# Two early expert items instead of four, six wide ones instead of four, and the last routing steps in larger portions

## The chip, the cores and the metric

The kernel runs on one core of a Trainium2 chip. Its engines work side by side, each through its own queue of instructions in order: TensorE (PE in the profile; PEld is its loading of weights), VectorE (DVE), ScalarE (ACT), GpSimd (POOL) and SyncE (SP). They wait for each other by semaphores. Transfers between DRAM and the on-chip memory are issued by SP (all the plain ones) and by GpSimd (those that take their addresses from a list: indirect ones, which gather or scatter rows). The metric is the device time of one execution in microseconds (us).

## What is computed

Two blocks behind each other. The first is a recurrence over 768 steps for 4 batches and 8 heads of 48 features; the second sends each of the 3072 rows to its two best of 8 experts.

```python
f = 1.0 / (1.0 + np.exp(-f_logit))
for t in range(S):
    state = f[:, :, t, :, None] * state + np.einsum('bhd,bhe->bhde', k[:, :, t], v[:, :, t])
    y[:, :, t] = np.einsum('bhd,bhde->bhe', q[:, :, t], state)
...
noisy_logits = x @ w_gate + np.log1p(np.exp(x @ w_noise)) * noise     # x: y as (3072, 384)
top2 = ...                                                            # the two largest of 8, softmax over them
for e in range(E):
    h = np.maximum(x[mask] @ w1[e], 0.0)                              # 384 -> 1024
    out[mask] += top2_w[mask, k, None] * (h @ w2[e])                  # 1024 -> 384
```

All of it is float32.

## The kernel before

**Attention.** The 768 steps are cut into 6 chunks of 128 (NCH), for 4 batches, so 24 blocks (NS). A loop runs over i from -3 to 25, and in each turn over seven stages that belong to different blocks (forget, scaled, scores, summed, output, decays, features). Each stage of each block is a *slot*. After features of the fourth batch of a chunk, `route(c)` is put at the end of a chain of generators, `router`. It holds the chunk's gating in some twenty small steps: soft-plus on ACT (L646 to L648), noise, maxima and their indices on DVE (L651 to L658), the softmax over two (L660 to L668), one-hot rows and counts (L673 to L685), ranks by two products on TensorE (L690, L691), and the slots in the lists (L694 to L699). Before the change each slot of the loop takes one step.

**Lists.** A row's place in its expert's list is known when its slot is. Then an *entry* (row, gate, token) is written to DRAM by an indirect DMA of GpSimd, `put` (L703), 128 rows at a time: 8 entries for a chunk, 48 in all. `puts` holds those that can go, and the loops take one from it now and then.

**Experts.** An expert's list is cut into *pairs* of 256 rows, 24 in all (three for each expert, 768 places; what goes beyond is done in five blocks of 32 rows, `quarter_block`). Before a pair can be worked on, SP *fetches* its list entries (L837, `slots`), GpSimd *gathers* the rows (L848, two halves of 128), and TensorE transposes them (L880, two groups of three to a pair). At its end GpSimd *scatters* two halves into the output, adding (L1141). Pairs are grouped into *items*:

- an *early* item is the first pair of an expert; its rows come from the first three chunks alone, so it can start before routing ends. Its first layer is plain (`first_layer`, L932), its second `second_layer` (L1198).
- a *narrow late* item holds the two other pairs of such an expert, 512 rows. The first layer saves products by sums of blocks (`first_of_two`, L957).
- a *wide late* item holds all three pairs of an expert that had no early one (`first_of_three`, L1094). Late second layers are `late_second_layer` (L1254).

Before, experts 0 to 3 have early items, and then come late 3 and 2 (narrow; their weights are still there), 4 to 7 (wide), 1 and 0 (narrow, their weights loaded again). Late items need complete lists: `fetch` of a late pair asserts that all 48 entries are issued, and on SP it waits until they have landed.

**Order.** Every item is a generator of *pieces*: an early one has 4 for the first layer (six products each) and 7 for the second (four products of 192 columns each); the transposes of the next item's pairs stand in pieces of the second layer, `between(1)` to `between(4)`, for the last early item one group in each of its pieces 5 to 8 (counted from 0). The first pieces run inside the attention loop; after it a loop takes the rest, and behind each piece come fetches, gathers, one or two router steps and up to as many entries. `in_order` fixes each engine's order as the order of tracing, so an instruction that waits holds up all behind it on its engine.

```python
most = min(NP if len(n_put) == NCH * B * 2 else NE, NP if what == "fetch" else done["fetch"])
```

This is in `ahead`: until all entries are issued, only early pairs may be fetched. The output is first filled with zeros by 24 DMAs of SP (L1461), 12 at the end of attention and one with each piece from the second item on.

Of the kernel before, what the change touches and what calls it, by code (L numbers as in the profile page):

```python
# [331 lines left out]
def kernel(  # L332
# [39 lines left out]
    B, H, S, D = q.shape  # L372
# [4 lines left out]
    NCH = S // C  # L377
# [6 lines left out]
    HALF = NCH // 2  # L384
    NP = 3 * E
    NI = 2 * E
    NE = 4
    WIDE = 4
    late_experts = (*range(NE - 1, NE - 3, -1), *range(NE, NE + WIDE), *range(NE - 3, -1, -1))
    items = [(e, [(e, 0)]) for e in range(NE)]  # L390
    items += [(e, [(e, 256 * i) for i in range(0 if e >= NE else 1, 3)]) for e in late_experts]
    pairs = [p for _, ps in items for p in ps]
    first_of = [sum(len(ps) for _, ps in items[:k]) for k in range(len(items) + 1)]
    assert NE + WIDE == E and len(pairs) == NP
    FH = FO // 2
# [94 lines left out]
    def load_router(part):  # L490

        if part < 2:
            for i, w in ((part, (moe_w_gate, moe_w_noise)[part]),):
                for odd in range(2):
                    for par in range(2):
                        nc.gpsimd.dma_start(out=w_rt[par * DP:par * DP + D, odd::2, XW + i * E:XW + (i + 1) * E],
                                          in_=w.rearrange("(a o r d) e -> o r d a e", o=2, r=2, d=D)[odd, par ^ odd])
        else:
            c = part - 2
            nc.sync.dma_start(out=noise[:, c], in_=moe_noise.rearrange("(b s) e -> s b e", b=B)[c * C:(c + 1) * C])  # L500
# [8 lines left out]
    xw, puts, n_put = [], [], []  # L509
# [8 lines left out]
    def load(nm, n):  # L518
        c, b = n // B, n % B
        if n < NCH * B:  # L520
            nc.sync.dma_start(out=pads[nm][n % RING[nm]][:, :, 0:D],
                              in_={"f": f_logit, "q": q, "k": k, "v": v}[nm][b, :, c * C:(c + 1) * C, :].rearrange("h t d -> t h d"))

    def clamp(n, engine=nc.gpsimd):
        if n < NCH * B:
            raw = pads["f"][n % RING["f"]][:, :, 0:D]
            engine.tensor_scalar(raw, raw, XMIN, None, ALU.max)
# [192 lines left out]
    def enough():  # L720
# [4 lines left out]
        yield  # L725
        lack = rt.tile([1, NE], F32, tag="lack", name="lack", bufs=1)
        nc.vector.tensor_scalar(lack, total[0:1, 0:NE], 255.5, None, ALU.is_lt)
        nc.vector.tensor_reduce(short, lack, axis=AX.X, op=ALU.max)
# [131 lines left out]
    def part_of_weights(k, which, part):  # L860
        if which == 1:
            few = slice(part * FF // 4, (part + 1) * FF // 4)
            nc.sync.dma_start(out=w1[k][:, :, few], in_=moe_w1[k].rearrange("(k p) f -> p k f", p=128)[:, :, few])
        else:
            few = slice(part * FO // 4, (part + 1) * FO // 4)
            nc.sync.dma_start(out=w2[k][:, few], in_=moe_w2[k].rearrange("(f p) d -> p f d", p=128)[:, few])
# [16 lines left out]
    done = {"fetch": 0, "gather": 0, 1: NR, 2: NR, "turned": False}  # L883
# [555 lines left out]
    def warm_up(count):  # L1439
        for _ in range(count):  # L1440
            nc.tensor.matmul(warm[:, 0:128], lhsT=ones, rhs=ones, start=True, stop=True)
# [15 lines left out]
    def zeros(count):  # L1457
        for _ in range(count):

            m = (*(m for m in range(NS) if m % NCH < HALF), *(m for m in range(NS) if m % NCH >= HALF))[len(zeroed)]  # L1460
            zeroed.append(nc.sync.dma_start(out=out[m * 128:(m + 1) * 128, :], in_=zero))  # L1461
            if m % NCH >= HALF:
                tc.declare_no_dep(zeroed[-1].ins, group="first half", reason="rows differ")
                tc.add_to_no_dep_group("second half", zeroed[-1].ins)
# [23 lines left out]
    def tables():  # L1488
        for i, val in enumerate((0, 0, FAR, 0)):
            nc.gpsimd.memset(empty[:, :, i], val)  # L1490
        nc.gpsimd.memset(entry, 0)
        for i, ids in ((0, row_of), (2, token)):
            nc.gpsimd.tensor_copy(entry[:, :, :, :, i], ids.unsqueeze(3).broadcast_to((128, NCH, B, 2)))
        nc.gpsimd.memset(zero, 0.0)

    router, first_pairs = iter(()), iter(())
    zeroed = []
    slot = n_routed = n_first = 0
    pieces = chain.from_iterable(((k, i) for i, _ in enumerate(first_layer(k) if k < NE else first_of_three(k) if is_wide(k) else first_of_two(k))) for k in range(len(items)))
    for i in range(-3, NS + 2):  # L1500
        order = [(forget, -3), (scaled, -1), (scores, 0), (summed, -2), (output, 1), (decays, -2), (features, 2)]
        if i < 0:
            order[0:2] = order[1::-1]
        for stage, lag in order:
            n = i - lag
            if not 0 <= n < NS:
                continue
            stage(n)
            if stage is forget:
                load("f", n + 4)  # L1510
                if n > 1:
                    clamp(n + 2)
                if n == 5:
                    tables()
            elif stage is scaled:
                for nm in "qk":
                    load(nm, n + 2) if n < 4 else load(nm, n + 3)
                    if n == 3:
                        load(nm, n + 3)
                if n in (1, 2):  # L1520
                    load_router(n - 1)
            elif stage is scores:
                for m in (n + 1,) if n < 4 else (2 * n - 3, 2 * n - 2) if n < 6 else (n + 3,):
                    load("v", m)
                if n in (2, 6, 7, 8, 9, 10):
                    load_router(2 + (2, 6, 7, 8, 9, 10).index(n))
                elif n == 5:
                    nc.sync.dma_start(out=lists.rearrange("(p r) w -> p r w", p=128), in_=empty)
            elif stage is output:
                while xw:  # L1530
                    xw.pop(0)()
                if 9 <= n < 17:
                    part_of_weights(0, 1 + (n - 9) // 4, (n - 9) % 4)
                elif n >= NS - 2:
                    part_of_weights(1, 1, 1 + (n - NS + 2) * 2)
            elif stage is features and n >= NS - 4:
                part_of_weights(1, 1, (n - NS + 4) * 2) if n < NS - 2 else zeros(4)
            next(router, None)
            slot += 1
            if puts and slot % (2 if n_routed == HALF else 3) == 0 and not (done["fetch"] and not done["gather"]):  # L1540
                puts.pop(0)()
            next(first_pairs, None)

            if done["turned"] and (n_first < 5 or i >= NS - 3 and stage is not forget) and (n_first < 11 or i >= NS - 1):
                next(pieces)
                n_first += 1
        if i < 0:
            warm_up(4)
        if i >= NS - 1:
            while xw:  # L1550
                xw.pop(0)()
        n = i - 2
        if n >= 0 and n % B == B - 1:
            c = n // B
            router = chain(router, route(c))
            n_routed = c + 1
            if c == HALF - 1:
                router = chain(router, enough())
                first_pairs = first_loads()
            if c == NCH - 1:  # L1560
                router = chain(router, plan(), beyond())
# [21 lines left out]
    for item, piece in pieces:  # L1583
        p = first_of[item] + max(0, piece - 8) // 7 if item >= NE else item
        if len(zeroed) < NS and item:
            zeros(1)
        ahead("fetch", p + 6)
        if piece % 2 == 0:
            ahead("gather", min(done["gather"] + 1, p + 3 if item < NE - 1 else first_of[min(item + 2, len(items))]))
        n = item - NE - 2  # L1590
        end = 7 + 7 * len(items[item][1])
        if 0 <= n < NQ:
            if piece == 9:
                quarter = quarter_block(n)
            if piece in (9, 10, 12, end - 1):
                next(quarter)
            if piece == 10:
                weights_quarter(n, 2)
        if 0 <= n + 1 < NQ:
            if piece in (13, 15):  # L1600
                (fetch_quarter if piece == 13 else gather_quarter)(n + 1)
            if piece == end:
                weights_quarter(n + 1, 1)
        for _ in range(1 if 3 <= piece < 7 else 2):
            next(router, None)
            if puts:
                puts.pop(0)()
    assert not puts and len(steer_q) == NI and next(router, quarter) is quarter and next(quarter, quarter) is quarter
# [40 lines left out]
```

## Time and profile before

| | us |
|---|---|
| median of 3 runs | 651.3 |
| lowest, highest | 649.95, 652.53 |
| the profiled execution | 653.94 |
| its span, from first to last instruction | 652.2 |
| TensorE busy | 633.4 (97%) |
| DVE busy | 440.9 (68%) |
| ACT busy | 290.1 (44%) |
| GpSimd busy | 269.0 (41%) |

The profile's span is a little shorter than the execution's own time, which also holds what lies before the first and behind the last instruction. Times in the views are counted from the span's start. Attention takes about the first 170 us; the early items stand from 166 to 250 us, the narrow ones behind them to 327, the four wide ones to 563, the last narrow ones to 644. A row of a timeline gives start, duration, engine, line, operation, what is written and read, the shapes and a count, and in brackets the idle time of the engine before it and what ended it. A row of the chain gives start, duration and name.

### The profile page before, as it was taken

How to read it: one execution, taken by the hardware profiler on the slowest of the kernel's cores; microseconds unless marked ns; L12 is line 12 of the kernel's file. 1: busy time of each engine (PE TensorE's matmuls, PEld its weight loads, DVE VectorE, ACT ScalarE, POOL GpSimd, SP SyncE). 2: the span in 40 equal slices, each digit the busy share in tenths (PEclk: the TensorE clock that was granted, in tenths of full speed). 3: DMA queues.
4: the chain of work that ended last, by engine and by line, in shares of the span. 5: the costliest groups of instructions: out<-in, count | busy, mean ns of one | idle time of the engine just before them, and what ended most of it. 6: DMA issues, size and time to landing. Idle time of an engine off the chain costs nothing.

```text
span 652.2 us, 13423 instructions
## 1 busy us (share of the span) xinstructions
PE 633.4 (97%) x5011; PEld 579.1 (89%) x5011; DVE 440.9 (68%) x1016; ACT 290.1 (44%) x763; POOL 269.0 (41%) x301
## 2 busy tenths in 40 slices
PE   7999999996999999999999999999999999999994
PEld 6999998884899999998988998898899889989894
DVE  6667877772475657659688678767867775574750
ACT  6777676651222133324366237425732762232220
POOL 7634697835246744052341435042433404232212
PEclk9899999996999999999999999999999999999998
DMA  9999987884989643245383557556463736645103
GB/s 181 182 213 197 185 178 146 176 204 119 282 262 224 167 74 73 98 92 162 90 268 121 126 96 217 178 76 205 94 201 46 236 117 131 156 134 123 23 5 49
DMA packets 153899, 96.33 MB, mean 148 GB/s; under 512 B 115600, under 2 KB 146320, under 8 KB 153824
## 3 DMA queue, kind: packets, MB, share of 16 engines
q1 hardware_dynamic: 141648, 76.12, 43.0%
q0 software_dynamic: 12176, 19.25, 17.3%
q8 instruction: 42, 0.69, 0.4%
q14 instruction: 33, 0.27, 0.1%
HBM read 75.97 MB, written 19.62 MB: 147 GB/s over the span
## 4 chain that ended last, share of the span: by engine, by line
PE 94%; DMA 2%; issue 2%; SPq 1%; POOL 1%; DVE 0%; ACT 0%; POOLq 0%
PE y L1254 27%; PE hp L932 6%; PE y L1198 6%; PE y L591 4%; PE E L1094 4%; PE D L1094 4%; PE xp L626 4%; PE sc L573 4%; PE C L1094 3%; PE P L957 3%; PE B L1094 3%; PE xgp L880 2%; PE y L602 2%; PE V L957 2%; PE W L957 2%; PE X L957 2%
## 5 line engine op out<-in xcount | busy, mean ns | idle before, releaser
L1141 POOL DMA_INDIRECT out_dram<-ys,slots x48 | 86.0, 1791 | 258.1 <-DVE ys L1260 185.0
L1254 PE MATMUL y<-qk_all,f_all 128*128 128x192 f32 x480 | 86.2, 327 | 0.0
L1254 PEld LDWEIGHTS y<-qk_all,f_all 128*128 128x128 f32 x480 | 77.2, 190 | 0.5 <-ACT ys L1270 0.3
L1260 DVE SCALAR_TENSOR_TENSOR ys<-y,slots,ys 128x192 f32<-128x192 f32 x60 | 24.9, 415 | 69.5 <-ACT ys L1279 29.7
L848 POOL DMA_INDIRECT xg<-x_rows,slots x48 | 51.0, 1063 | 44.7 <-DMA slots<-lists 23.4
L1254 PE MATMUL y<-w,hs_b 128*128 128x192 f32 x320 | 58.6, 326 | 0.0
L703 POOL DMA_INDIRECT lists<-entry,sloti x48 | 53.0, 1104 | 10.3 <-issue 9.7
L1254 PEld LDWEIGHTS y<-w,hs_b 128*128 128x128 f32 x320 | 53.1, 190 | 0.4
L980 ACT ACTIVATE hs_b<-hs_b 128x256 f32<-128x256 f32 x64 | 25.9, 417 | 52.4 <-DVE hs_b L977 47.4
L932 PE MATMUL hp<-xt_a,w 128*128 128x256 f32 x192 | 42.4, 380 | 0.0
L1303 ACT ACTIVATE ys<-y,slots 128x192 f32<-128x192 f32 x20 | 8.4, 421 | 74.8 <-PE y L1254 74.8
L576 DVE TENSOR_TENSOR A<-sc,causal 128x1024 f32<-128x1024 f32 x24 | 29.3, 1222 | 16.6 <-PE sc L573 9.7
L932 PEld LDWEIGHTS hp<-xt_a,w 128*128 128x128 f32 x192 | 36.2, 190 | 4.7
L1102 ACT ACTIVATE hs_b<-hs_b 128x256 f32<-128x256 f32 x80 | 33.5, 418 | 6.0 <-DVE hs_b L1106 4.9
L606 ACT COPY yT<-y 128x256 f32<-128x256 f32 x48 | 15.7, 375 | 45.7 <-PE y L602 32.2
L591 PE MATMUL y<-A,v_all 128*64 128x128 f32 x384 | 29.5, 293 | 2.1 <-issue 2.1
L547 DVE TENSOR_TENSOR_SCAN L<-f,cap 128x512 f32<-128x512 f32 x24 | 29.5, 1229 | 0.6 <-ACT cap L542 0.6
L1254 PE MATMUL y<-qk_all,hs_b 128*128 128x192 f32 x160 | 29.8, 329 | 0.0
L1254 PE MATMUL y<-w,f_all 128*128 128x192 f32 x160 | 29.8, 329 | 0.0
L573 PE MATMUL sc<-qP,kQ 64*128 64x128 f32 x384 | 28.4, 288 | 0.0
L626 PE MATMUL xp<-w_rt,yT 128*128 128x112 f32 x192 | 28.4, 292 | 0.0
L1254 PEld LDWEIGHTS y<-qk_all,hs_b 128*128 128x128 f32 x160 | 26.2, 190 | 2.1 <-issue 2.1
(279 smaller groups left out, 1539.8 us busy)
## 6 DMA issues: line engine op xcount, KB each, us to landing
w<-in_moe_w_dram SPq DMA_DIRECT2D x16, 1536.0 KB
w_q<-in_moe_w_dram SPq DMA_DIRECT2D x10, 1536.0 KB
w<-in_moe_w_dram SPq DMA_DIRECT2D x16, 384.0 KB
f_all<-in_f_logit_dram SPq DMA_DIRECT2D x24, 192.0 KB
qk_all<-in_q_dram SPq DMA_DIRECT2D x24, 192.0 KB
qk_all<-in_k_dram SPq DMA_DIRECT2D x24, 192.0 KB
v_all<-in_v_dram SPq DMA_DIRECT2D x24, 192.0 KB
x_rows<-xs SPq DMA_DIRECT2D x24, 192.0 KB
```

Of the source, the lines that this page charges most:

```text
L573: nc.tensor.matmul(sc[:, par, cols(hp)], lhsT=kQ[n][rows(par), cols(hp)], rhs=qP[n][rows(par), cols(hp)], start=True, stop=True)
L591: nc.tensor.matmul(at(hp, par), lhsT=vt[:, 2 * hp + par, :], rhs=A[n][:, par, cols(hp)], start=(hp < 2), stop=(c == 0 and hp >= HP - 2))
L626: nc.tensor.matmul(xp[:, hp, :], lhsT=yT[n][:, hp % 2, cols(hp // 2)], rhs=w_rt[:, hp, :], start=True, stop=True)
L703: into = nc.gpsimd.indirect_dma_start(out=lists, out_offset=bass.IndirectOffsetOnAxis(ap=sloti[:, r, b:b + 1], axis=0), in_=entry[:, c, b, ...
L848: nc.gpsimd.indirect_dma_start(out=xg[p][:, s, :], out_offset=None, in_=x_rows[0:HALF * B * C] if p < NE else x_rows, in_offset=bass.Indir ...
L932: nc.tensor.matmul(hp[:, o, :], lhsT=w1[home(k)][:, i, (fo + o) * 128:(fo + o + 1) * 128], rhs=xt_a[:, i, k % 2 * 256:(k % 2 + 1) * 256], ...
L957: nc.tensor.matmul(to, lhsT=x, rhs=y, start=start, stop=stop, skip_group_check=goes_on)
L1094: nc.tensor.matmul(banks[name, j], lhsT=half_of(x, k)[:, j * 128:(j + 1) * 128], rhs=half_of(y, k), start=first, stop=True, skip_group_che ...
L1102: nc.scalar.activation(at(to, j), at(y, j), AF.Relu, scale=-1.0 if more[0][0] == "-" else 1.0)
L1141: into = nc.gpsimd.indirect_dma_start(out=out, out_offset=bass.IndirectOffsetOnAxis(ap=slots[p][:, s, 2:3], axis=0), in_=ys[s], in_offset= ...
L1198: nc.tensor.matmul(P[name], lhsT=x[:, o, :], rhs=y[:, o, :], start=(o == 0), stop=(o == FH - 1))
L1254: nc.tensor.matmul(to, lhsT=x[:, o, :], rhs=y[:, o, :], start=(start and o == 0), stop=(o == FH - 1), skip_group_check=not start)
```

## The change

Only experts 0 and 1 keep an early item. The order of the late items becomes 1, 0 (narrow, weights still there), then 2 to 7 (wide). So there are ten items instead of twelve, and 22 early pieces instead of 44.

In the attention loop the router makes two steps a slot once chunk 4 is under way, and entries are taken every second slot in the last two chunks (every third before). In the loop behind it, the router makes four steps behind a piece until all 48 entries are there to be taken (one or two before), and two entries are taken behind every piece (one behind the pieces 3 to 6 before).

```diff
-    NE = 4
-    WIDE = 4
+    NE = 2
+    WIDE = 6
...
-            next(router, None)
+            for _ in range(2 if n_routed >= NCH - 1 else 1):
+                next(router, None)
             slot += 1
-            if puts and slot % (2 if n_routed == HALF else 3) == 0 and not (done["fetch"] and not done["gather"]):
+            if puts and slot % (2 if n_routed in (HALF, NCH - 1, NCH) else 3) == 0 and not (done["fetch"] and not done["gather"]):
                 puts.pop(0)()
...
-        for _ in range(1 if 3 <= piece < 7 else 2):
+        routed = len(n_put) + len(puts) == NCH * B * 2
+        for _ in range(1 if routed and 3 <= piece < 7 else 2 if routed else 4):
             next(router, None)
+        for _ in range(2):
             if puts:
                 puts.pop(0)()
```

## The prediction

> **What bounds the kernel now.** First the page of the profile: its span, the slices and the chain that ended last.
>
> ```profile
> span 652.2 us, 13423 instructions
> ...
> PE   7999999996999999999999999999999999999994
> ...
> PEclk9899999996999999999999999999999999999998
> ...
> PE 94%; DMA 2%; issue 2%; SPq 1%; POOL 1%; DVE 0%; ACT 0%; POOLq 0%
> ```
>
> TensorE is the bound: 94% of the chain is PE, nearly every slice shows nine tenths, and the granted clock dips visibly in one place, near 150 us. So a product taken away is worth its full time, and a TensorE wait that is added costs its full time. Second, the windows of two wide items, TensorE alone (us of the window, busy us and count, clock, DMA share, GB/s):
>
> ```profile
> 327.41:386.59 59.18, 59.18 (x401) 1.00 0.55 150
> 386.59:445.77 59.18, 59.18 (x401) 1.00 0.57 149
> ```
>
> Wide items leave TensorE no gap, and wide behind wide costs the same each time, with DMA, DVE and ACT at hand. So six in a row should run as four do.
>
> **The products: -6.9 us.** First layers, in the chain and in windows of their own lines (two records to a product):
>
> ```profile
> 187.88 10.36 PE hp L932 x48
> ...
> 249.70:270.10 20.40, 19.24 (x88) 16.52 (x88) 1.00 0.35 65
> 327.40:353.35 25.95, 25.94 (x120) 22.53 (x120) 1.00 0.58 183
> ```
>
> An early item needs 24 products of 256 columns in 10.36 us, 0.432 each; a narrow late item needs 44, a wide one 60 (25.94 / 60 is again 0.432). Two experts change from 24 + 44 products to 60: 2 x 8 x 0.432 = 6.9 us less. The second layer has seven groups of four products per 256 rows either way, and the transposes stay 48 groups. Two experts' weights are no longer loaded twice: four DMAs go from SP. TensorE did not wait for them, so on the path that is nothing by itself.
>
> **What the change uncovers.** A late item needs complete lists. Before, between the last chunk's ranks and the first late transposes stood the end of the second, the whole third and half of the fourth early item. Now the ranks (L690) come in the first early item and the first late transposes in the sixth piece of the second. Counted along the loops, all 48 entries are issued by the end of the first early item, with both its scatters among the last eight. The chain is ranks, slots, entries, fetch, gather, transposes; I price it link by link.
>
> *Inside the attention loop* the router now makes two steps a slot for chunk 4. I cost that at nothing: DVE and ACT wait for TensorE there. If that cover were gone, it would be the 3.9 us of small DVE instructions counted next.
>
> *Ranks.* The last chunk's steps, one or two to a piece before, come four to a piece: soft-plus in the third piece, ranks in the seventh.
>
> ```profile
> 175.12 0.60 ACT L934 ACTIVATE hs_a<-hp 128x512 f32<-128x512 f32 x1 [1.99 <-issue]
> ...
> 187.23 0.21 ACT L646 ACTIVATE sp<-lg 128x32 f32<-128x32 f32 x1
> ...
> 187.74 0.23 ACT L648 ACTIVATE sp<-sp 128x32 f32<-128x32 f32 x1
> ```
>
> ```profile
> 186.64 0.18 DVE L694 TENSOR_TENSOR at<-rk,list_of 128x32 f32<-128x32 f32 x1
> ...
> 187.56 0.17 DVE L699 CAST sloti<-slot 128x8 uint32<-128x8 f32 x1 [0.18 <-DVE slot L698]
> ...
> 188.37 0.18 DVE L651 SCALAR_TENSOR_TENSOR sp<-lg,sp 128x32 f32<-128x32 f32 x1
> ...
> 192.10 0.94 DVE L904 TENSOR_TENSOR qk_all<-w,qk_all 128x768 f32<-128x768 f32 x1
> 193.72 0.69 DVE L1129 TENSOR_TENSOR f_all<-hs_a 128x512 f32<-128x512 f32 x1 [0.69 <-ACT hs_a L934]
> ...
> 202.48 0.24 DVE L685 TENSOR_TENSOR_SCAN upto<-carry,each 128x40 f32<-128x40 f32 x1
> ```
>
> ```profile
> 198.24 2.60 PE y L1198 x16
> 200.84 0.33 PE xgp L880 x3
> ...
> 205.40 0.14 PE rk L690 x2
> 205.54 0.22 PE rk L691 x2
> ```
>
> The third piece's Relu ended at 175.7; chunk 4's ranks (0.14 + 0.22) now stand ahead of this item, so 176.1. Three ACT steps (187.23 to 187.97, 0.74) bring 176.8. Then DVE, in order: 24 small instructions from L651 to L685, at about 0.16 each 3.9 us; between them one L904 (0.94), two L1129 (1.38), and as estimates a turn's copy (0.5) and the trip to ACT for an exponential (0.3). Sum 7.0: the ranks' operands are ready at 183.8. TensorE would come there at 187.88 less four groups of 1.30 and a turn of 0.33, 182.3. It waits 1.5 us, and with it every product behind. Ends: 0, if DVE gets ahead, and 2.5. With the ranks (0.36), a hop of 0.25 and L694 to L699 (1.09) the slots are there at 185.5.
>
> *Entries, fetch, gather.* GpSimd works in order:
>
> ```profile
> 187.26 1.62 POOL L1141 DMA_INDIRECT out_dram<-ys,slots  x1 [12.39 <-DMA w<-in_moe_w_dram]
> ...
> 209.28 1.69 POOL L1141 DMA_INDIRECT out_dram<-ys,slots  x1 [4.38 <-ACT ys L1226]
> 211.28 1.64 POOL L703 DMA_INDIRECT lists<-entry,sloti  x1 [0.30 <-DVE step_plan L746]
> ...
> 217.64 0.96 POOL L703 DMA_INDIRECT lists<-entry,sloti  x1 [0.23 <-issue]
> ...
> 224.29 0.96 POOL L703 DMA_INDIRECT lists<-entry,sloti  x1 [0.22 <-issue]
> ...
> 231.02 1.35 POOL L848 DMA_INDIRECT xg<-x_rows,slots  x1 [5.69 <-DMA slots<-lists]
> ```
>
> SP's timeline, SP's waits, and a window of the DMA share:
>
> ```profile
> 228.43 2.95 SPq L837 DMA_DIRECT2D slots<-lists  x6
> ```
>
> ```profile
> SPq L837 <- DMA lists<-entry,sloti: 14.3, 1, 14.3
> ```
>
> ```profile
> 233.00:234.00 1.00, 0.69 (x2) 1.00 0.68 197
> ```
>
> An entry takes 1.3 (217.64 to 224.29 is five of them), the first one behind a scatter 1.9 (1.64 and the 0.3 behind it), a scatter 2.0 (209.28 to 211.28). Chunk 4's slots are written before the third piece; even from its Relu at 175.1, eight entries end by 185.5. From there: three entries, 189.4; the first scatter (187.26, now 2.0 later for the ranks and their wait), 191.4; four entries, 197.2; the second scatter, 199.2. There the last entry is issued. Its landing is what SP's fetch waits for: 4.1 later (224.29 to 228.43), 203.3. Fetch to gather is 2.6: 205.9. Half a gather is 128 rows of 1536 bytes, 197 KB, moved by the end of the window that closes 3.0 after its start: 208.9. As a check, 211.28 to 231.02 are 19.7 us with one scatter inside, and my 20.4 holds two.
>
> TensorE comes to its transposes at 200.84, plus 0.5 for ranks and total now ahead of them, plus 1.5: 202.8. It waits **6.1 us**. Low end 4.0: a landing as short as fetch to gather, and nothing extra behind scatters. High end 8: two more us, as 1.64 in place of 0.96 for three of the entries would give. The three turns that follow come 1.63 apart, as fast as gathers are issued (about 1.3 to 1.65), so nothing is added.
>
> *Beside the gather.* The zero writes of the second early item, 192 KB each, stand on SP behind the fetch, ten of them, and are issued all at once when it is released. I add 0.4 (0 to 1).
>
> *Clock.* A wait also lowers the granted clock:
>
> ```profile
> 16.33 0.63 PE L533 MATMUL kp<-ident,qk_all 128*128 128x128 f32 x4 [2.13 <-DMA qk_all<-in_k_dram]
> ...
> 148.05 0.46 PE L591 MATMUL y<-A,v_all 128*64 128x128 f32 x4
> ...
> 159.53 2.05 PE L626 MATMUL xp<-w_rt,yT 128*128 128x112 f32 x8
> ```
>
> ```profile
> 18.00:21.00 3.00, 3.00 (x32) 0.50 1.06 208
> ```
>
> ```profile
> 163.00:164.50 1.50, 1.50 (x20) 0.50 0.73 205
> ```
>
> An idle time of 2.13 us was followed by 3 us at 0.50, and after the slow stretch near 150 TensorE, busy again from 159.5, still ran at 0.50 until 164.5. Half of 3 to 5 us is 1.5 to 2.5; I take 2.0. The Trainium skill (TensorE: Matmul & The Clock Gate, Part 1) gives half clock after an idle window of about 3.4 us and full clock after about 3.4 us of steady work: by it the sum has 1.7 here, and nothing if the wait stays under 3.4. The trace halved after less.
>
> **Sum:** -6.9 + 1.5 + 6.1 + 0.4 + 2.0 = +3.1 us. The profiled execution took 653.94 (span 652.2), so 657.0 by its own time; the median of the runs, 651.3, lies 0.4% under it, and the same step gives **654.4 us**. By the ends: -6.9 + 0 + 4.0 + 0 + 1.5 = -1.4 and -6.9 + 2.5 + 8 + 1 + 2.5 = +7.1, so this case's own range is 649.9 to 658.4. A measurement tells about 0.5%, 3.3 us, from no change: the forecast is no change that it can tell, with the larger part of the rest on the slow side.
>
> **Rivals.**
>
> *The cover is enough.* The lists arrive before TensorE needs them: 651.3 - 6.9 = 644.4, or 645.9 with the wait for the ranks. For it: no weight loads run beside the entries any more. Against: entries to gather took 19.7 us, where 17 now lie from slots to transposes. 0.14.
>
> *The gather starves behind the zeros (slower).* Ten zeros and the one of the next piece are 2.1 MB, 5.4 us at 392 GB/s:
>
> ```profile
> 206.00:208.00 2.00, 0.00 (x0) 1.00 1.03 392
> ```
>
> A gather before, its second half here, and the queues from 199.7 to 206 us, beside zeros and a weight load (SP's q1, GpSimd's q0: packets, MB, share):
>
> ```profile
> 200.03 0.95 POOL L848 DMA_INDIRECT xg<-x_rows,slots  x1 [0.30 <-issue]
> ```
>
> ```profile
> q1 hardware_dynamic: 300, 1.23, 80.3%
> q0 software_dynamic: 29, 0.11, 4.4%
> ```
>
> Only 0.11 of the gather's 0.39 MB moved. If the first gather lands only behind the zeros, the wait grows by 5 more: 659.4; from 0.2 us above my sum it counts as slower. Against: entries and a scatter stood ahead of those gathers on q0, and none will here. The Trainium skill (DMA: Bandwidth & Descriptors, Queues, rings and completion order) has each DMA engine alternate between its queues packet by packet; that would leave about the 0.4, and the rows above lean the other way. 0.12.
>
> *The slow stretch near 150 does not come back.* Products that elsewhere take under 2 us last there from 148.05 to 159.53, with no wait shown. Without it and its half clock some 12 us go from my sum: 642. Against: three runs from 649.95 to 652.53, too close together for something that comes and goes. 0.08.
>
> **Chances.** Forecast 0.64 (within 0.5% 0.38, slower 0.24, faster 0.02); cover enough 0.14 (faster 0.12, same 0.02); starved 0.12, slower; no stretch 0.08, faster; 0.02 for anything else, same. Faster 0.22, same 0.42, slower 0.36. The range 645 to 660 leaves out the stretch and half of the first rival.
>
> **What would show it.** Products: L932 x96, and 720 records on L1094. Ranks: a TensorE wait before L690 near 182, released by L685. Lists: a wait before L880 near 203, released by the gather; SP's fetch near 203, behind the last entry; the clock near 0.5 just after. If the fetch comes before 197, my links are too dear and the first rival holds. If the gather lands much over 3 us after its issue, the zeros did it. If a wide item takes over 59.2, six in a row were not free.

## The result, and the profile after

| | before | after |
|---|---|---|
| median, us | 650.62 (4 runs) | 659.23 (4 runs) |
| lowest, highest | 648.98, 652.53 | 656.41, 659.61 |
| ratio of after to before | | 1.0121, 95% interval 1.0091 to 1.0151 |
| profiled execution, its span | 653.94, 652.2 | 659.61, 657.8 |

The change makes the kernel slower by 1.2%. The range 645 to 660 held the time, by 0.8 us; the sum's own range, 649.9 to 658.4, did not, and the forecast, no change that can be told, did not come true. The page of the kernel after, its span, slices and chain:

```profile
span 657.8 us, 13492 instructions
...
PE   8999999895995999999999999999999999999995
...
PEclk9999999996998899999999999999999999999999
...
PE 85%; DMA 5%; issue 4%; POOL 3%; ACT 1%; SPq 1%; DVE 1%; POOLq 0%; DVEq 0%; ACTq 0%
```

TensorE's share of the chain fell from 94% to 85%, and DMA, GpSimd and "issue" came in. The slices show two hollows, near 155 and near 208 us, where before showed one. Behind the second hollow nearly everything runs as forecast. Windows of TensorE from wide item to wide item (us of the window, busy us and count, clock, DMA share, GB/s), and the first layer of the early items:

```profile
300.46:359.64 59.18, 59.18 (x401) 1.00 0.55 150
...
478.00:537.18 59.18, 59.18 (x401) 1.00 0.56 149
537.18:596.56 59.38, 59.38 (x401) 1.00 0.47 121
```

```profile
L932 PE MATMUL hp<-xt_a,w x96: 378/379/462, 168.4 to 201.3; 128*128 128x256 f32 x96
```

Four of the six wide items take the 59.18 us of before and the fifth 59.38, a little over the 59.2 at which the prediction would have doubted itself; the sixth ends the kernel. Only half of the early first layers are left. So the 6.9 us of products were saved but for about 0.2. What these rows show as lost lies ahead of the first late item, and most of it is in one chain. The waits of TensorE from 130 to 240 us, then the chain from the last chunk's slots on:

```profile
PE xgp L880 <- DMA xg<-x_rows,slots: 7.3, 1, 7.3
...
PE rk L691 <- DVE each L681: 0.8, 1, 0.8
```

```profile
186.85 0.96 POOL lists L703
...
190.71 1.62 POOL out_dram L1141
...
197.31 1.39 POOL lists L703
199.00 1.61 POOL out_dram L1141
200.92 4.06 DMA lists<-entry,sloti
205.00 1.75 DMA slots<-lists
207.56 3.96 DMA xg<-x_rows,slots
211.61 0.90 PE xgp L880 x3
```

This is the chain that the prediction built link by link: last entry forecast 199.2 and measured 200.92, fetch 203.3 and 205.00, gather 205.9 and 207.56. The gaps between links were right (landing 4.1 and 4.06, fetch to gather 2.6 and 2.56), except the last: gather to transposes took 4.05 and not 3.0. TensorE came at 204.29 (forecast 202.8). Both ends of the wait came about 1.6 us late, because the first early item started at 168.4 and not at 166.2 as in before; their difference came out near the forecast. The clock around this wait, TensorE alone:

```profile
204.30:207.60 3.30, 0.00 (x0) 1.00 0.13 4
207.70:211.60 3.90, 0.00 (x0) 0.50 0.84 245
211.70:217.90 6.20, 6.20 (x23) 0.50 0.90 318
218.00:219.00 1.00, 1.00 (x9) 1.00 0.01 2
```

It fell about 3.4 us after TensorE went idle, and the first 6.2 us of work behind the wait ran at 0.50: 3.1 us lost, where 2.0 were forecast.

So the sum of what these rows show is -6.9 + 0.8 + 7.3 + 3.1 = +4.3 us, and the medians differ by 8.6. The rest, 4.3 us, had no place in the prediction's sum. In the profiled executions 2.2 us lie ahead of all this: the first early item starts at 168.4 in place of 166.2 (0.4 of it are chunk 4's ranks, which stood inside that item before). Windows of TensorE there, before and then after:

```profile
145.00:150.00 5.00, 4.16 (x56) 1.00 0.62 194
150.00:155.00 5.00, 2.34 (x11) 0.59 0.60 96
155.00:160.00 5.00, 3.32 (x16) 0.50 0.59 186
```

```profile
145.00:150.00 5.00, 4.83 (x67) 1.00 0.71 234
150.00:155.00 5.00, 2.62 (x12) 0.81 0.65 172
155.00:160.00 5.00, 2.32 (x8) 0.50 0.33 110
160.00:165.00 5.00, 3.27 (x20) 0.50 0.03 11
```

Both kernels have a slow stretch at the end of attention, in which TensorE has few products running and no wait that the profile can name, and half clock. In after it holds on for longer. GpSimd's timeline beside it gave a suspect: in both kernels GpSimd issues indirect DMAs back to back through the stretch. The last one of that run in before, and in after:

```profile
156.13 0.97 POOL L703 DMA_INDIRECT lists<-entry,sloti  x1 [0.23 <-issue]
```

```profile
159.51 0.97 POOL L703 DMA_INDIRECT lists<-entry,sloti  x1 [0.23 <-issue]
```

The run holds ten of them from 144.52 before, and twelve from 145.35 after; TensorE's last unexplained gap ends at 158.16 and 162.43. That became the theory to test: the larger steps put more entries into that run, and TensorE is slow for as long as it lasts. The rival: the stretch has its own cause, and the steps cost time elsewhere.

### The profile page after: what moved, and what is told of

Read it like the earlier page. It is cut to its first block, busy times and chain, and to the rows that moved or that the text cites. A ratio compares the mean times of both kernels' runs of the same rounds, so it can differ in the third digit from the quotient of the medians.

```text
span 657.8 us, 13492 instructions
## 1 busy us (share of the span) xinstructions
PE 630.1 (96%) x4979; PEld 575.5 (87%) x4979; DVE 456.0 (69%) x1056; ACT 312.9 (48%) x839; POOL 272.6 (41%) x301
## 4 chain that ended last, share of the span: by engine, by line
PE 85%; DMA 5%; issue 4%; POOL 3%; ACT 1%; SPq 1%; DVE 1%; POOLq 0%; DVEq 0%; ACTq 0%
PE y L1254 29%; PE E L1094 6%; PE D L1094 6%; PE B L1094 5%; PE C L1094 5%; PE xp L626 4%; PE y L591 4%; PE sc L573 3%; PE xgp L880 2%; PE y L602 2%; POOL lists L703 2%; PE A L1094 2%; PE P L957 2%; PE y L1198 1%; PE kp L533 1%
## 5 line engine op out<-in xcount | busy, mean ns | idle before, releaser
L1254 PE MATMUL y<-qk_all,f_all 128*128 128x192 f32 x528 | 94.4, 327 | 0.0
L1254 PEld LDWEIGHTS y<-qk_all,f_all 128*128 128x128 f32 x528 | 84.9, 190 | 0.2
L1254 PE MATMUL y<-w,hs_b 128*128 128x192 f32 x352 | 64.4, 326 | 0.0
L1254 PEld LDWEIGHTS y<-w,hs_b 128*128 128x128 f32 x352 | 58.4, 190 | 0.4
L1102 ACT ACTIVATE hs_b<-hs_b 128x256 f32<-128x256 f32 x120 | 50.2, 418 | 8.4 <-DVE hs_b L1106 7.2
L880 PE MATMUL xgp<-ident,xg 128*128 128x128 f32 x144 | 24.7, 283 | 7.3 <-DMA xg<-x_rows,slots 7.3
L626 PEld LDWEIGHTS xp<-w_rt,yT 128*128 128x128 f32 x192 | 24.5, 195 | 7.5 <-issue 6.9
L527 POOL TENSOR_SCALAR f_all<-f_all 128x384 f32<-128x384 f32 x22 | 27.9, 1272 | 5.4 <-DMA f_all<-in_f_logit_dram 5.4
L1129 DVE TENSOR_TENSOR f_all<-hs_b 128x512 f32<-128x512 f32 x44 | 29.9, 683 | 0.0
L1254 PEld LDWEIGHTS y<-w,f_all 128*128 128x128 f32 x176 | 28.9, 190 | 0.7
```

The source lines that it names most:

```text
L626: nc.tensor.matmul(xp[:, hp, :], lhsT=yT[n][:, hp % 2, cols(hp // 2)], rhs=w_rt[:, hp, :], start=True, stop=True)
L880: nc.tensor.transpose(xp[:, i * 128:(i + 1) * 128], xg[p][:, s, i * 128:(i + 1) * 128], ident)
L1102: nc.scalar.activation(at(to, j), at(y, j), AF.Relu, scale=-1.0 if more[0][0] == "-" else 1.0)
L1129: nc.vector.tensor_tensor(sm[which], x, y, op)
L1254: nc.tensor.matmul(to, lhsT=x[:, o, :], rhs=y[:, o, :], start=(start and o == 0), stop=(o == FH - 1), skip_group_check=not start)
```

## The experiments

Each was timed beside runs of the kernel before on its own chip. Medians there: 649.82 (29 runs) for the first four, 649.43 (18) for the next four, 649.68 (16) for the last four.

### The larger steps alone

```diff
 kernel after
-    NE = 2
-    WIDE = 6
+    NE = 4
+    WIDE = 4
```

> The changed kernel with four early and four wide items again, so that only the larger routing and entry steps are left of the change. Theory (the lists come too late for the first late item, because two early items cover too little): the list wait before L880 is gone, as four early items cover it; what stays is a wait of about 0.8 us before the last chunk's ranks (L691) and the slow stretch near 150 us that lasted some 2 us longer: ratio to before 1.002 to 1.006. Rival (the larger steps do no harm at all, everything lost is the list wait): 1.000. Rival (the larger steps cost TensorE or DVE several us in the first early item): 1.008 or more.

Measured: 656.07 us, ratio 1.0107 (1.0061 to 1.0152). With the items of before, the larger steps alone make nearly all of the slowdown: 0.0107 x 649.8 = 7.0 us, of which the trace shows 0.8 as the wait for the ranks. There is no wait ahead of L880. The rival that the steps cost several us held, against my own expectation. The profiled execution took 652.29, near the lowest of six (651.73 to 660.0), so its trace cannot show where the rest of the 7 us lies.

### Three early items

```diff
 kernel after
-    NE = 2
-    WIDE = 6
+    NE = 3
+    WIDE = 5
```

> The changed kernel with three early and five wide items. Theory: one expert's products are saved (3.5 us) and the third early item, about 20.7 us of TensorE work, stands between ranks and late transposes, more than the 7.3 us that were missing, so no list wait and no half clock there: -3.5 + 0.8 (ranks) + 2 (slow stretch) = about -0.7 us, ratio 0.995 to 1.001. Rival (fewer early items and more wide ones in a row cost by themselves): halfway between before and the change, about 1.006.

Measured: 652.87 us, ratio 1.0048 (1.0019 to 1.0077). One expert's products go (-3.5 us), no late wait comes, and still it is slower than before. The rival's 1.006 lies in the interval, my 0.995 to 1.001 outside it. But that rival would have fewer early items cost something by themselves, and with the same larger steps three early items come out 0.0059 or 3.8 us below four, about what their products save; what both share is the larger steps. Its trace has a wait of 2.3 us for the ranks, and the slow stretch.

### The first late item on lists that are there early

```diff
 kernel after
-        if p < NE:
+        if p < NE + 2:
...
-        row = pairs[p][0] * N + pairs[p][1]
+        row = pairs[p - NE if NE <= p < NE + 2 else p][0] * N + pairs[p - NE if NE <= p < NE + 2 else p][1]
```

> The changed kernel, but the first narrow late item fetches the entries and gathers the rows of the two early pairs instead of its own (its own rows are left out, the work is the same), which are complete long before. Theory: the wait before L880 near 204 us and the half clock behind it disappear: -6.9 + 0.8 (ranks) + 2 (slow stretch) = -4 us, ratio 0.991 to 0.996, and the second late item, fetched from the complete lists, does not wait. Rival (the wait for the lists moves to the next late item): a wait of several us before the transposes of the second late item, ratio over 1.0.

The first late item's own rows are left out here. Measured: 650.94 us, ratio 0.9994 (0.9967 to 1.0021), so 0.0127 or 8.2 us less than after's ratio. The rows of after give 7.3 + 3.1 = 10.4 for the wait and the half clock behind it; a wait of 3.1 us with 3.3 us of half clock behind it remained, worth 4.7, since the next gathers stand behind the last entry on GpSimd. That leaves 5.7 of the 8.2; in the two traces the surplus lies ahead of the items, which start at 163.2 here and at 168.4 in after. My expected 0.991 to 0.996 had no such remainder in it.

### The scatters behind the last entry

```diff
 kernel after
+    held = []
...
+            held.append(partial(add_rows, s)) if k == 0 else add_rows(s)
+
+        def add_rows(s):
...
+        while held and len(n_put) == NCH * B * 2:
+            held.pop(0)()
```

The first early item's two scatters are kept back until the last entry is issued.

> The changed kernel with the first early item's two scatters issued behind the last list entry instead of among the last eight. Theory (GpSimd's order is the chain): the last entry is issued 3.9 us earlier after the ranks, so SP's fetch and the gather come 3.9 us earlier, the wait before L880 falls from 7.3 to about 3.4 us and the half clock behind it shortens by 1 to 3 us at half price: 4 to 5.5 us less than the change, ratio to before 1.003 to 1.007. Rival (the landing of entries or the zero writes set the gather, not GpSimd's order): the wait stays near 7 us, ratio 1.012.

Measured: 650.75 us, ratio 1.0017 (0.9994 to 1.0040); the wait ahead of the transposes is 3.05 us in place of 7.32. So the two scatters in the queue of GpSimd do delay the lists, by the 4 us that the prediction counted for them. The time fell by more than the wait, (1.0121 - 1.0017) x 650 = 6.8 us, but the intervals of the two ratios leave room for 4.3. In the two traces the surplus lies ahead of the items: the first starts at 164.8 here and at 168.4 in after.

### No entries in the stretch

The kernel before with one condition more.

```diff
 kernel before
-            if puts and slot % (2 if n_routed == HALF else 3) == 0 and not (done["fetch"] and not done["gather"]):
+            if puts and i < NS - 3 and slot % (2 if n_routed == HALF else 3) == 0 and not (done["fetch"] and not done["gather"]):
```

> The kernel before, except that no entry is issued in the attention loop from the pair-head i = 21 on; those entries come in the piece loop instead. In before GpSimd issues about ten indirect DMAs (gathers and entries) back to back from 144.5 to 156.1 us, and TensorE's slow stretch beside it ends near 158.2. Theory (TensorE is slowed for as long as that run of indirect DMAs lasts): the run falls to about four DMAs and ends some 5 us earlier, the clock's half stretch there shrinks or goes, and the attention ends 3 to 6 us earlier: ratio 0.990 to 0.995 if nothing is given back in the pieces. Rival (the stretch has another cause, such as the early lists' own wait): it stays as long as it is, ratio 0.998 to 1.002. A third reading: the entries that were held come late in the pieces, and a wait for the late lists takes back what was won: then the trace shows a wait ahead of L880 near 205 us.

Measured: **639.52 us, ratio 0.9863** (0.9838 to 0.9887). It is the fastest of all, and faster than both kernels of this case. TensorE in the windows of the stretch, and GpSimd's timeline:

```profile
145.00:150.00 5.00, 5.00 (x75) 1.00 0.83 266
150.00:155.00 5.00, 5.00 (x46) 1.00 0.92 305
155.00:160.00 5.00, 5.00 (x27) 1.00 0.94 317
```

```profile
140.25 0.95 POOL L848 DMA_INDIRECT xg<-x_rows,slots  x1 [0.30 <-issue]
156.58 1.01 POOL L848 DMA_INDIRECT xg<-x_rows,slots  x1 [15.38 <-DMA slots<-lists]
```

The run of indirect DMAs is four long and ends at 141.2; TensorE shows one gap of 0.21 us, no half clock, and the slow stretch is gone. The traffic itself is not what slowed TensorE: from 150 to 155 us the DMA engines are busier here (0.92) than in before (0.60). The first early item starts here at 151.9, where before it starts at 166.2:

```profile
L932 PE MATMUL hp<-xt_a,w x192: 379/379/462, 151.9 to 224.8; 128*128 128x256 f32 x192
```

```profile
L932 PE MATMUL hp<-xt_a,w x192: 379/379/463, 166.2 to 239.1; 128*128 128x256 f32 x192
```

Of these 14.3 us, 3.0 stand ahead of the stretch already (GpSimd's last L618 starts at 137.7 and 134.7). The gain can be read from the trace of before. Its clock:

```profile
150.00:151.00 1.00, 0.42 (x3) 0.97 0.03 1
151.00:155.00 4.00, 1.93 (x8) 0.50 0.75 119
...
164.50:166.00 1.50, 1.50 (x26) 0.97 0.96 294
```

From about 151.0 to 164.6 us the clock is at half, and TensorE is busy for 9.8 us of that, which cost 4.9. With the 5.1 us of gaps this makes 10.0; the medians differ by 9.9.

### Half of the hold

```diff
 the kernel above
-            if puts and i < NS - 3 and slot % ...
+            if puts and i < NS - 2 and slot % ...
```

> The kernel before with no entry issued in the attention loop from i = 22 on, one pair-head later than in the run that gave 0.9863. Theory (TensorE's slow stretch lasts as long as GpSimd's run of indirect DMAs behind its first few): the run is between four and ten DMAs long, and the ratio lies between the two, 0.989 to 0.996, with the last gap of TensorE some 2 us behind the run's end. Rival (it is the holding from i = 21 that counts, say because a certain head must not have them): 0.998 to 1.002 or 0.986 with nothing between.

Measured: 644.36 us, ratio 0.9902 (0.9879 to 0.9926), between the two as the theory has it. The run is six long, its last gather, and TensorE's last gap:

```profile
143.06 0.96 POOL L848 DMA_INDIRECT xg<-x_rows,slots  x1 [0.30 <-issue]
```

```profile
145.05 1.75 PE L591 MATMUL y<-A,v_all 128*64 128x128 f32 x13 [0.34 <-issue]
```

Over the kernels, from the profiled executions: GpSimd's run (DMAs with under 0.6 us between them), TensorE's gaps over 0.2 us, and the time from the start of GpSimd's last L618 to the first L932. The kernels have the same products in it, but for 0.4 us of ranks that the attention-loop edits move there:

| kernel | run of indirect DMAs, us | DMAs | gaps, us | sum, us | L618 to L932, us |
|---|---|---|---|---|---|
| before | 144.5 to 157.1 | 10 | 148.8 to 158.2 | 5.1 | 28.5 |
| piece-loop edits alone | 136.4 to 148.9 | 10 | 142.0 to 150.7 | 5.0 | 26.8 |
| larger steps alone | 139.7 to 153.8 | 11 | 146.9 to 155.5 | 4.9 | 27.6 |
| attention-loop edits alone | 136.9 to 150.8 | 11 | 142.6 to 151.8 | 5.9 | 28.1 |
| after | 145.4 to 160.5 | 12 | 151.1 to 162.4 | 6.7 | 30.6 |
| half of the hold | 136.5 to 144.0 | 6 | 142.2 to 145.0 | 1.7 | 22.2 |
| no entries | 136.3 to 141.2 | 4 | 141.9 | 0.2 | 17.2 |

The gaps begin 4 to 7 us into a run and end about 1 to 2 us behind it, wherever the run ends. The other kernels fit: three more with the hold have four DMAs and 16.7 to 18.1 us, two with eleven 27.9 and 28.5, two with twelve 29.6 and 30.2. The second row has the attention loop of before word for word, and yet its first early item starts at 161.3 and not at 166.2, so single traces differ by some us here, and steps of one or two DMAs are near that difference.

### The two halves of the larger steps

The kernel before with the attention-loop edits of the change alone, and with the piece-loop edits alone.

```diff
 attention loop
-            next(router, None)
+            for _ in range(2 if n_routed >= NCH - 1 else 1):
+                next(router, None)
...
-            if puts and slot % (2 if n_routed == HALF else 3) == 0 ...
+            if puts and slot % (2 if n_routed in (HALF, NCH - 1, NCH) else 3) == 0 ...
 piece loop
-        for _ in range(1 if 3 <= piece < 7 else 2):
+        routed = len(n_put) + len(puts) == NCH * B * 2
+        for _ in range(1 if routed and 3 <= piece < 7 else 2 if routed else 4):
             next(router, None)
+        for _ in range(2):
```

> The kernel before with the attention-loop edits of the change alone (two router steps after each unit once seven chunks are routed, entries on every second slot), four early and four wide items, pieces as before. All larger steps together gave 1.0107 with four early items, of which a rank wait of 0.8 us is 0.0013. Theory (the attention loop's edits cost what the prediction put at nothing, by a longer run of indirect DMAs near 150 us): ratio 1.005 to 1.010. Rival (the excess is made in the piece loop): 0.998 to 1.002.

(The second router step begins with five chunks routed, `NCH - 1`, not seven.)

> The kernel before with the piece-loop edits of the change alone (four router steps and two entries after a piece until all entries are built), the attention loop as before. Theory (the excess is made in the attention loop): 0.998 to 1.002, with at most a wait for the ranks of about 1 us. Rival (the pieces' larger steps put router work in TensorE's way): 1.005 to 1.010.

Measured: 651.81 us, ratio 1.0036 (1.0021 to 1.0052), and 651.95 us, ratio 1.006 (1.0028 to 1.0093). Both cost something. The sum, 0.0096, is that of the larger steps together, 0.0107, within the intervals. The attention-loop half is 2.3 us, where the prediction put nothing; its point lies below my 1.005 to 1.010. The piece-loop half is 3.9 us, of which a wait ahead of L690 is half:

```profile
182.41 0.38 PE L690 MATMUL rk<-each,earlier 128*128 128x32 f32 x2 [1.98 <-DVE xt_a L881]
```

So my theory, that all of it is made in the attention loop, was half right, and the rival for the pieces, 1.005 to 1.010, held. In the trace of the attention-loop edits, two gaps of 1.2 us with no releaser also stand in the pieces, at 182 and 204 us, each at the end of a run of ten and twelve indirect DMAs.

### The hold with the attention-loop edits

```diff
 attention-loop edits alone
-            if puts and slot % ...
+            if puts and i < NS - 3 and slot % ...
```

> The kernel before with the attention-loop edits (which alone gave 1.0036) and no entry issued in the attention loop from i = 21 on (which alone gave 0.9863). Theory (what the attention-loop edits cost is the longer run of indirect DMAs, and the router steps themselves stand beside TensorE's products for nothing): ratio 0.985 to 0.988, as without the edits. Rival (the second router step per unit costs time itself): 0.989 to 0.992, the 0.0036 added back.

Measured: ratio 0.9891 with an interval of 0.9838 to 0.9944, which holds the theory's values and the rival's. Single executions lay from 638.96 to 651.48 us, so the time decides nothing. The trace, of an execution of 650.93, shows more. The hold works: the run is four long, and TensorE is busy without a gap from 140 to 160 us. But in the pieces GpSimd now has twenty-one indirect DMAs back to back (176.6 to 207.0), and TensorE's waits from 120 to 240 us are

```profile
PE hp L932 <- issue: 5.8, 5, 1.8
PE y L1198 <- DVE mx L657: 2.6, 1, 2.6
```

The five gaps, which nothing releases, lie between 199.9 and 208.0 us in an early item's first layer, with half clock from 204 on, and the second wait is one for the router's own DVE work. So gaps of this kind also come beside the early items' longer products, and the second router step can cost a wait; how often, one trace cannot show.

### Three early items with the hold

Once with the larger steps, once with every step as in before.

```diff
 three early items, larger steps
-            if puts and slot % ...
+            if puts and i < NS - 3 and slot % ...
```

```diff
 no entries in the stretch
-    NE = 4
-    WIDE = 4
+    NE = 3
+    WIDE = 5
```

> Three early and five wide items with the larger steps (which alone gave 1.0048), and no entry issued in the attention loop from i = 21 on. Theory (the run of indirect DMAs lengthens the slow stretch): the 4 to 5 us that the larger steps cost there go, while the products keep their gain of 3.5 us: ratio 0.990 to 0.996. Rival (the stretch has another cause): 1.003 to 1.007, as without the hold. If the held entries make the late lists late, a wait ahead of L880 shows it, with its length to be taken off.

> Three early and five wide items with every step as in the kernel before, and no entry issued in the attention loop from i = 21 on. With four early items the last entry ended at 211.0 us there and the gather behind it began at 216.2; three early items end near 157 + 61.5 = 218.5. Theory (the early items' cover is just enough without the larger steps, so the 3.5 us of products come on top of 0.9863): ratio 0.979 to 0.984. Rival (the lists come late): a wait ahead of L880 of 3 to 6 us with half clock behind it, ratio 0.986 to 0.993.

Measured: 644.97 us, ratio 0.9918 (0.9895 to 0.9942) with the larger steps, and 646.63 us, ratio 0.9953 (0.9939 to 0.9967) with the small ones. The first agrees with the theory: the hold takes 0.013 from 1.0048, though its trace has two gaps of 0.8 us in the pieces. The second lands beyond the rival: the lists come too late, TensorE's wait being

```profile
PE xgp L880 <- DMA xg<-x_rows,slots: 7.5, 1, 7.5
```

I had put the attention's end at 157 us, and 3 to 6 us for the wait. In the kernel with the hold the items start at 151.9; TensorE asks for the lists sooner, and what the cover lacks grows by as much. Neither beats four early items with the hold.

### Zero writes ahead

```diff
 kernel after
-    zeros(4)
+    zeros(16)
```

> The kernel after, with the zero writes that stand on SP behind the late fetch (eleven of them, 207.5 to 214.5 us) issued ahead of the early items. Theory (they share the DMA engines with the late items' first gather and cost it about 1 us): the wait ahead of L880 falls from 7.3 to about 6.3 us and the ratio is 1.008 to 1.012 against before. Rival (the zeros cost the gather nothing, or they cost as much where they now stand): the wait stays at 7.3 us, ratio 1.011 to 1.015. A rival that the prediction held against the change (the gather starves behind the zeros) would show 3 us less or more.

Measured: the wait ahead of L880 fell from 7.3 to 6.2 us, as expected:

```profile
PE xgp L880 <- DMA xg<-x_rows,slots: 6.2, 1, 6.2
```

The zeros beside the first gather cost it about 1.1 us; they do not starve it. The ratio, 1.0068 (1.0047 to 1.0089), lies below what was expected and is 0.0053 or 3.4 us under after's. The clock makes up part: it is at half from 203.7 to 210.5 us, but TensorE works in only 3.1 us of that, in place of 6.2, which is 1.6 us less lost. With the 1.1 this is 2.7; the rest lies within the intervals.

## Why the prediction was right, and where not

**Products, -6.9 us: right.** L932 x96, 59.18 us for each of the first four wide items and 59.38 for the fifth, so next to no loss from six in a row.

**Ranks, +1.5 us: right in kind, 0.8 in size.** The wait stood at L691, released by DVE, at 185.08. Against the start of the item, the chain of DVE was priced about 1 us too long, and TensorE came 0.2 us earlier.

**Lists, +6.1 us and +0.4 for the zeros: right.** The wait was 7.3 us. Taking the zeros away leaves 6.2, the forecast's 6.1, so the mis-sized term is the zeros: about 1.1, where 0.4 was taken and 1 was the upper end. That two scatters among the last eight entries hold the lists up was shown by moving them: 3.05 us left. The rival of a gather that starves needed 5 us more and got 0.7 (1.1 less 0.4); the rival that the cover is enough fell with the wait itself.

**Clock, +2.0 us: right in kind, 3.1 in size.** The estimate was half of 3 to 5 us at half clock; 6.2 us were worked at it. The Trainium skill (TensorE: Matmul & The Clock Gate, Part 1) gives half clock after at least one idle window of about 3.4 us, and here the fall came 3.4 us into the wait. But with the zeros ahead it came 2.5 us in, and two shorter waits halved the clock as well, 3.05 us with the scatters moved and 3.1 on early lists:

```profile
200.60:203.40 2.80, 0.07 (x1) 1.00 1.05 328
203.50:210.20 6.70, 6.47 (x23) 0.50 0.86 314
```

```profile
206.40:209.70 3.30, 3.30 (x14) 0.50 1.01 351
209.80:212.00 2.20, 2.20 (x15) 1.00 1.01 363
```

So a wait under 3.4 us is no safe price of nothing, and half clock held for 3.3 us in one kernel and for 6.7 in the other.

**Inside the attention loop, "at nothing": this step failed.** Alone, the attention-loop edits cost 2.3 us (0.0021 to 0.0052 of 649). I asked whether DVE and ACT have room for the second router step, and did not count what the edit to `puts` issues: more entries on GpSimd in the same stretch. That they act by lengthening the run of indirect DMAs is likely but not shown: from L618 to L932 a run of ten has 26.8 and 28.5 us, of eleven 27.6 to 28.5, of twelve 29.6 to 30.6 (0.4 less in the last two without the ranks), so twelve are slower, while ten and eleven overlap; and the trace of these edits alone, with eleven, also has 2.4 us of gaps in the pieces. Nor did I price the piece loop's larger steps beyond their wait for the ranks: 3.9 us alone, about 2 more than that wait; where these lie in the trace is not shown.

**"The stretch does not come back": its price was nearly right, its cause overlooked.** The prediction put the stretch at some 12 us, as something that might stay away by itself. With the entries kept out of it, it is gone, and 9.9 us with it. The prediction had the 11.5 us from 148.05 to 159.53 in a quoted row, "with no wait shown", and looked no further at what the other engines did in them.

Together: the forecast's own terms, as measured, come to 4.3 us in place of 3.1, and the medians differ by 8.6. The profiled executions differ by less (657.8 - 652.2 = 5.6), 2.2 us of it ahead of the first early item (0.4 of them the moved ranks) and 3.4 behind it, where the terms' 4.3 leave nothing unexplained. Before's profiled execution lies 3.3 us above its median, and no trace shows where an execution nearer the median is faster. The missing 4.3 us are therefore put down to the larger steps by their time alone, 7.0 us (4.0 to 9.9) with the ranks' 0.8 among them; these intervals are too wide to share it out further between the loops.

## What to carry to other kernels

A stretch in which the bounding engine has gaps that no semaphore explains is the first thing to test, by moving what the other engines issue there; here one condition was worth 1.4%, more than the change tried to win. When a loop's step is enlarged, count everything the step issues, DMAs first, and not only whether the engines that compute have room. Work taken away ahead of a chain of DMAs is won only up to the chain's slack, and every us won earlier in the kernel makes that slack smaller.

## What the runs showed of the hardware

TensorE lost up to 6.7 us in gaps beside GpSimd's back-to-back indirect DMAs at the end of attention: 0 to 0.9 with four of them, 1.7 with six, 4.7 to 6.7 with ten to twelve. The gaps in after:

```profile
152.48 0.41 PE L602 MATMUL y<-qP,st 64*64 64x128 f32 x2 [0.46 <-issue]
153.89 1.09 PE L602 MATMUL y<-qP,st 64*64 64x128 f32 x5 [1.00 <-issue]
155.33 0.69 PE L602 MATMUL y<-qP,st 64*64 64x128 f32 x3 [0.35 <-issue]
156.75 0.58 PE L602 MATMUL y<-qP,st 64*64 64x128 f32 x2 [0.73 <-issue]
158.17 0.57 PE L626 MATMUL xp<-w_rt,yT 128*128 128x112 f32 x2 [0.36 <-issue]
```

Work resumes every 1.41 to 1.44 us, in a rhythm of its own, near that of the DMAs on GpSimd (1.26 to 1.31 apart). But a run alone is not enough: in the kernel with the hold, ten such DMAs from 156.6 us and twelve from 174.1 stand beside the early items' longer products, and TensorE has no gap over 0.2 us there. Nor do longer products keep the gaps away: beside a run of twenty-one (one execution of the hold with the attention-loop edits) there were 5.8 us of them, and at the end of two runs of ten and twelve (the attention-loop edits alone) 1.2 us each. What passes between GpSimd and TensorE in such a run, and whether it is the issuing or the small transfers themselves, no run here shows.
